# Spectra with real and imaginary parts on the rows, 16-bit phases, and the skip term by GpSimd and TensorE

## The chip, the core and the metric

One Trainium2 chip, of which the kernel uses one core. A core has five engines that run their own instruction queues in order: TensorE (PE, with its weight loads shown apart as PEld), VectorE (DVE), ScalarE (ACT), GpSimd (POOL) and SyncE (SP), which here only issues transfers. They meet through semaphores. The metric is the time of one execution on the device in microseconds.

## What is computed

The forward and the backward pass (the vector-Jacobian product for `grad_out`) of one block. `A_u` has 2048 rows of 512 in bf16; the state-space part has 128 states for each of the 512 channels; the dense part is 512 to 1792 to 512.

```python
def _A_ref(u, A_re, A_im, B_re, B_im, C_re, C_im, log_dt, Dskip):
    dt = jnp.exp(log_dt)[:, None]
    logdA = dt * (A_re + 1j * A_im)
    dB = dt * (B_re + 1j * B_im)
    P = jnp.exp(logdA[:, :, None] * l[None, None, :])
    K = jnp.einsum("dn,dnl,dn->dl", Cc, P, dB).real
    Kf, Uf = rfft2(pad(K)), rfft2(pad(u.transpose(0, 2, 1)))
    y = irfft2(Uf * Kf)[..., :L].transpose(0, 2, 1) + u * Dskip
    return y

xn = _layernorm(A_u)
s = _A_ref(xn, ...)
g = _silu(_silu(xn @ w1) @ w2)
out = A_u + s * g
```

The outputs are `out` and the gradients for `A_u`, the six state-space arrays, `log_dt`, `Dskip`, `w1` and `w2`.

## The kernel before

The convolution along the 2048 rows is done as a discrete Fourier transform by matmuls, in four blocks `b` of 128 channels. `dft_fwd` makes a spectrum in three steps: s1 (32 matmuls, line 298) over the first factor of the length, a turn by 32 PE transposes (line 304), and s2 (line 314) over the second. A spectrum is a tile of 128 rows x 4096: in the free direction `c` (real, imaginary), 16 groups `g` and 128 columns `k`. In s2 the real and the imaginary part come from two matrices of 64 columns, `F2[:, 0]` and `F2[:, 1]`; each matmul fills 64 rows of the PSUM tile, one group `h` on the upper and one on the lower half. `cplx_mul` (lines 340 to 354) multiplies two spectra on DVE, in two halves of five or six instructions with a help tile `cm2`. `dft_inv` goes back: i2 (line 327) with two accumulated matmuls for each group, 256 columns wide, and i1 (line 336) with two for each of the 16 steps `t`; a function `consume` takes each half of the result out of PSUM.

The stages stand in this order. The set-up loads x and the parameters, normalises, and builds constants (`make_consts`). Then `chain()` runs, block by block, the tables of the state-space kernel (`gen_tables`), the spectrum of x (`gen_conv_x`) and, one block behind, the forward convolution (`gen_conv_fwd`), while the dense forward pass (`gen_ffn_fwd`, ps_h and ps_o) is paced beside it. `gen_tables` makes its sines from integer phases `V`: a product (line 433), a shift by a quarter turn (435), a shift of bits (436) that throws away whole turns, and the sine on ACT (438). `gen_conv_fwd` reloads the spectrum of x (`spectrum_in`), stores its own (`KXd`), multiplies, and in `consume` adds the skip term xn * Dskip (lines 543, 544) on DVE. The last forward block runs beside the gates (`gen_gate_rows`). Then come the backward convolutions (`gen_conv_bwd`): `forward(b)` makes the spectrum `dA` of ds, and `rest(b)` loads both stored spectra and multiplies `dA` by each, with an inverse transform for each; the FFN's backward pass (`gen_ffn_da`, ps_da, dhT, ps_dx) and the output rows (`gen_out`) run beside it. The state-space gradients and the weight gradients follow.

The program is written as generators that are interleaved; a scheduler then orders each engine's queue by dependences and priority before the run, and at run time every queue is strict. Transfers are issued in order by SP (most), by GpSimd (stores of hT, ob and the outputs, `k.st`) and by ACT (a few). Spectra live in pool tiles with tag `w8` (4 buffers, and 2 more, `w8b`, in the backward stage); PSUM tiles for the convolutions (`pc`) have two buffers. `evc` casts on ACT (line 44), `evq` copies on DVE (line 45).

Of the kernel before, what the change touches and what calls it, by code (L numbers as in the profile page):

```python
# [14 lines left out]
I32 = mybir.dt.int32  # L15
DRAM = bass.MemoryType.DRAM
PSUM = bass.MemoryType.PSUM
P = 128
PI_LO = 3.1415925
PB = 18  # L20
# [113 lines left out]
def make_consts(k, wp):  # L134
# [11 lines left out]
    c8 = wp.tile([P, 16, 8], I32, name="c8")  # L146
    G.iota(c8[:], pattern=[[1, 16], [0, 8]], base=0, channel_multiplier=0)
    c4 = wp.tile([P, 16, 4], I32, name="c4")
    G.iota(c4[:], pattern=[[1, 16], [0, 4]], base=0, channel_multiplier=0)
    e8 = wp.tile([P, 16, 8], I32, name="e8")  # L150
    G.iota(e8[:], pattern=[[0, 16], [1, 8]], base=0, channel_multiplier=0)
# [21 lines left out]
    pt, ph, pe, pg = (wp.tile([P, 1], I32, name=nm) for nm in ("p_t", "p_h", "p_e", "p_g"))  # L173
# [4 lines left out]
    nc.vector.scalar_tensor_tensor(out=pg[:], in0=ph[:], scalar=4.0, in1=pe[:], op0=ALU.mult, op1=ALU.add)  # L178
# [4 lines left out]
    TT(out=kf[:, 0], in0=flat(c4), in1=pt[:].to_broadcast([P, 64]), op=ALU.mult)  # L183
    TT(out=kf[:, 1], in0=kf[:, 0], in1=sh[:, 1:2].to_broadcast([P, 64]), op=ALU.add)
    TT(out=kf[:, 0], in0=kf[:, 0], in1=sh[:, 0:1].to_broadcast([P, 64]), op=ALU.add)
    TS(out=kf[:], in_=kf[:], scalar=15, op=ALU.bitwise_and)
    kk = wp.tile([P, 128], I32, name="kk")
    TT(out=kk[:], in0=flat(c8), in1=pt[:].to_broadcast([P, 128]), op=ALU.mult)
    mask = wp.tile([P, 128], F32, name="mask")
    TT(out=mask[:], in0=flat(e8), in1=pg[:].to_broadcast([P, 128]), op=ALU.is_equal)  # L190
    maskf = wp.tile([P, 64], F32, name="maskf")
    TT(out=maskf[:], in0=flat(e4), in1=pe[:].to_broadcast([P, 64]), op=ALU.is_equal)
    kq = wp.tile([P, 3, 128], I32, name="kq")
    for i, shift in enumerate((12, 8, 0)):
        TS(out=kq[:, i], in_=kk[:], scalar=shift, op=ALU.add)
    TS(out=kq[:], in_=kq[:], scalar=15, op=ALU.bitwise_and)
    sf = wp.tile([P, 2, 64], F32, name="sf")
    nc.scalar.activation(out=sf[:], in_=kf[:], func=ACT.Sin, scale=2.0 * math.pi / 16.0, bias=k.mpi[:])
    sv = wp.tile([P, 3, 128], F32, name="sv")
    nc.scalar.activation(out=sv[:], in_=kq[:], func=ACT.Sin, scale=2.0 * math.pi / 16.0, bias=k.mpi[:])  # L200
# [6 lines left out]
    TT(out=sv[:], in0=sv[:], in1=mask[:].unsqueeze(1).to_broadcast([P, 3, 128]), op=ALU.mult)  # L207
    k.I2 = const.tile([P, 2, 2, 128], BF16, name="I2")
    TS(out=k.I2[:, 0], in_=sv[:, 0:2], scalar=2.0 / 4096, op=ALU.mult)
    TS(out=k.I2[:, 1, 0, :], in_=sv[:, 2], scalar=2.0 / 4096, op=ALU.mult)  # L210
    TS(out=k.I2[:, 1, 1, :], in_=sv[:, 0], scalar=2.0 / 4096, op=ALU.mult)
# [76 lines left out]
def dft_fwd(k, w8, U, ev):  # L288
# [19 lines left out]
    Bv = B[:].rearrange("p u (g h) k -> p u h g k", h=2)  # L308
    for u in range(2):
        for c in range(2):  # L310
            ps = pc.tile([P, 8, P], F32, name="ps_s2", tag="pc")
            for v in range(2):
                for h in range(2):
                    nc.tensor.matmul(out=ps[64 * h:64 * h + 64, 4 * v:4 * v + 4], lhsT=k.F2[:, c, :], rhs=Bv[:, u, h, 4 * v:4 * v + 4, :],  # L314
                                     start=True, stop=True)
            ev(A[:, c, 8 * u:8 * u + 8, :], ps[:])
# [3 lines left out]
def dft_inv(k, A2, Y, ev, consume):  # L320

    nc, pc = k.nc, k.pc
    for g0 in range(0, 16, 4):
        ps = pc.tile([P, 4, 32, 8], F32, name="ps_i2", tag="pc")
        for g in range(4):
            for c in range(2):
                nc.tensor.matmul(out=ps[:, g], lhsT=Y[:, c, g0 + g, :], rhs=k.I2[:, c].rearrange("p c m -> p (c m)"),  # L327
                                 start=(c == 0), stop=(c == 1))
        ev(A2[:].rearrange("p c t (g e) -> p g (c t) e", e=8)[:, g0:g0 + 4], ps[:])
    yield  # L330
    for h in range(2):
        ps = pc.tile([P, 8, P], F32, name="ps_i1", tag="pc")
        for j in range(8):
            t = 8 * h + j
            for c in range(2):
                nc.tensor.matmul(out=ps[:, j], lhsT=k.TI[:, 2 * t + c, :], rhs=A2[:, c, t, :], start=(c == 0), stop=(c == 1))
        consume(8 * h, 8, ps)


def cplx_mul(k, w8, a, b, conj=False):  # L340

    TT = k.nc.vector.tensor_tensor
    n = 8
    for g0 in range(0, 16, n):
        gs = slice(g0, g0 + n)
        t2 = w8.tile([P, 2, n, P], BF16, name="cm2", tag="cm2")
        TT(out=t2[:, 0], in0=b[:, 1, gs], in1=a[:, 1, gs], op=ALU.mult)
        TT(out=t2[:, 1], in0=b[:, 0, gs], in1=a[:, 1, gs], op=ALU.mult)
        TT(out=b[:, :, gs], in0=b[:, :, gs], in1=a[:, 0:1, gs].to_broadcast([P, 2, n, P]), op=ALU.mult)
        TT(out=b[:, 0, gs], in0=b[:, 0, gs], in1=t2[:, 0], op=ALU.add if conj else ALU.subtract)  # L350
        if conj:
            TT(out=b[:, 1, gs], in0=t2[:, 1], in1=b[:, 1, gs], op=ALU.subtract)
        else:
            TT(out=b[:, 1, gs], in0=b[:, 1, gs], in1=t2[:, 1], op=ALU.add)

# [155 lines left out]
def spectrum_in(k, w8, b, which):  # L511
    t = w8.tile([P, 2, 16, P], BF16, name="sp_in", tag="w8")
    k.nc.sync.dma_start(t[:].rearrange("p c g k -> p (c g k)"), {"U": k.Ud, "K": k.KXd}[which][b])
    return t
# [701 lines left out]
```

## Time and profile before

| | |
|---|---|
| median of 3 runs | 702.68 us (699.33 to 708.69) |
| span of the profiled execution | 703.6 us |
| PE busy | 597.5 us (85%) |
| DVE busy | 534.5 us (76%) |
| ACT busy | 465.3 us (66%) |
| GpSimd busy | 85.6 us (12%) |
| moved by DMA | 148.81 MB, 211 GB/s on average |
| mean granted TensorE clock | 0.958 |

Busy times are from the hardware profiler's record of one execution. The durations of single instructions are used from that execution, so sums are held against its span and not against the median. A matmul's mean duration includes the time through the array, in which the next is already running; the union of busy time divided by the count is nearer to what one costs. A busy share over the whole span mixes stages with different limits.

### The profile page before, as it was taken

To read this page: it belongs to the slowest core of one execution; us is meant where nothing else is said; L and a number is where in the kernel's file an instruction comes from. 1 tells how busy PE (TensorE), PEld (TensorE's weight loads), DVE (VectorE), ACT (ScalarE), POOL (GpSimd) and SP (SyncE) were. 2 spreads that over 40 slices of the span, in tenths; PEclk is the share of its full clock that TensorE was granted. 3 is DMA by queue.
4 is the path that set the end of the run, shared out by engine and by line. 5 is a ranking of instruction groups with operands and counts; after the bars stand their busy time and mean duration, and the time that the engine had idled before them with its cause. 6 is when DMAs were issued, how large, how long until landed. Compare 5 with 4: busy or idle time off the path is not lost.

```text
span 703.6 us, 14464 instructions
## 1 busy us (share of the span) xinstructions
PE 597.5 (85%) x5884; PEld 436.8 (62%) x5884; DVE 534.5 (76%) x952; ACT 465.3 (66%) x626; POOL 85.6 (12%) x165
## 2 busy tenths in 40 slices
PE   0675988779999997549988999988998989999988
PEld 0454656466667675337675666756777767755877
DVE  6988995979979958999685969626679774755950
ACT  6877666779878888877664765615728665645431
POOL 2355200000000000000000000000001020123220
PEclk9998998899999999779999999999999999999999
DMA  9955453825835779598857545479989999337993
GB/s 280 342 139 201 150 192 143 329 77 211 306 120 217 288 245 310 175 295 264 275 166 226 184 172 180 129 155 226 249 202 252 197 235 232 110 116 254 288 229 99
DMA packets 158771, 148.81 MB, mean 211 GB/s; under 512 B 79280, under 2 KB 136112, under 8 KB 155120
## 3 DMA queue, kind: packets, MB, share of 16 engines
q1 hardware_dynamic: 145664, 125.07, 62.3%
q0 software_dynamic: 6144, 17.83, 6.7%
q10 hardware_dynamic: 6896, 4.98, 2.2%
q8 instruction: 46, 0.75, 0.4%
q14 instruction: 21, 0.17, 0.1%
HBM read 65.14 MB, written 64.36 MB: 184 GB/s over the span
## 4 chain that ended last, share of the span: by engine, by line
issue 74%; POOL 8%; DVE 8%; PE 4%; DMA 4%; ACT 1%; SPq 0%; POOLq 0%; DVEq 0%
PE ps_w L986 2%; POOL Hd L575 1%; DMA dh_tok<-DHd 1%; DVE st L269 1%; POOL out_dram L842 1%; POOL rstd L273 1%; DVE jk L1019 1%; POOL SEL L220 1%; DVE o L1029 1%; DMA out_dram<-gout 1%; PE ps_o L583 1%; DMA out_dram<-o 1%; DVE xn L279 1%; POOL out_dram L971 1%; PE ps_h L566 1%
## 5 line engine op out<-in xcount | busy, mean ns | idle before, releaser
L44 ACT CAST dA<-ps_s 128x1024 bf16<-128x1024 f32 x96 | 93.6, 1027 | 16.2 <-PE ps_s L298 10.2
L925 PE MATMUL ps_da<-doT,W 128*128 128x256 bf16 x448 | 62.5, 280 | 5.7 <-DVE dhT L927 5.7
L44 ACT CAST dB<-ps_i 128x1024 bf16<-128x1024 f32 x48 | 47.3, 1027 | 29.2 <-PE ps_i L327 24.4
L772 DVE TENSOR_TENSOR Tp<-Vb,Eb 128x1344 bf16<-128x1344 bf16 x64 | 51.9, 853 | 18.5 <-ACT Vb L44 7.9
L927 DVE TENSOR_TENSOR dhT<-ps_da,dhT 128x512 bf16<-128x512 f32 x56 | 37.8, 686 | 34.2 <-PE ps_da L925 29.3
L566 PE MATMUL ps_h<-XT,W 128*128 128x256 bf16 x448 | 62.1, 284 | 0.6 <-DVE XT L45 0.4
L583 PE MATMUL ps_o<-W,aT 128*128 128x512 bf16 x224 | 56.9, 390 | 3.5 <-ACT aT L574 1.6
L327 PE MATMUL ps_i<-I,sp_in 128*128 128x256 bf16 x384 | 51.4, 279 | 8.0 <-DVE sp_in L350 4.9
L936 PE MATMUL ps_dx<-W,dhT 128*128 128x512 bf16 x224 | 54.1, 379 | 0.0
L925 PEld LDWEIGHTS <-W 128*128 128x128 bf16 x448 | 43.0, 100 | 16.7 <-issue 10.8
L986 PE MATMUL ps_w<-dh_tok,xn 128*128 128x256 bf16 x448 | 49.7, 272 | 3.6 <-DMA dh_tok<-DHd 3.5
L968 PE MATMUL ps_w<-YD,a_tok 128*128 128x512 bf16 x224 | 51.5, 379 | 0.0
L566 PEld LDWEIGHTS <-W 128*128 128x128 bf16 x448 | 43.2, 102 | 12.3 <-issue 5.5
L986 PEld LDWEIGHTS <-xn 128*128 128x128 bf16 x448 | 43.6, 98 | 9.8 <-issue 4.5
L327 PEld LDWEIGHTS <-sp_in 128*128 128x128 bf16 x384 | 36.7, 100 | 20.9 <-DVE sp_in L350 8.2
L44 ACT CAST Vb<-ps_v 128x672 bf16<-128x672 f32 x64 | 42.3, 725 | 10.7 <-PE ps_v L762 10.6
L44 ACT CAST o<-ps_w 128x256 bf16<-128x256 f32 (+1 forms) x42 | 17.7, 439 | 46.4 <-PE ps_w L986 16.9
L314 PE MATMUL ps_s<-dB,F 128*64 128x512 bf16 x192 | 33.6, 418 | 12.2 <-DVE dB L45 6.5
L298 PEld LDWEIGHTS <-TF 128*128 128x128 bf16 x384 | 26.7, 102 | 24.4 <-issue 18.6
L583 PEld LDWEIGHTS <-aT 128*128 128x128 bf16 x224 | 21.3, 100 | 29.4 <-issue 9.3
L45 DVE COPY dB<-pt_f 128x2048 bf16<-128x2048 bf16 x24 | 28.7, 1218 | 12.5 <-PE pt_f L304 12.4
L472 PE MATMUL ps_k<-W,YD 128*128 128x84 bf16 x512 | 29.4, 210 | 9.6 <-DVE W L467 7.7
(231 smaller groups left out, 1304.5 us busy)
## 6 DMA issues: line engine op xcount, KB each, us to landing
Yd<-YD SPq DMA_DIRECT2D x8, 1024.0 KB, 4.5
sp_in<-Ud SPq DMA_DIRECT2D x8, 1024.0 KB, 7.4
h_in<-Hd SPq DMA_DIRECT2D x14, 512.0 KB, 4.3
Ed<-E SPq DMA_DIRECT2D x8, 672.0 KB, 4.1
Eb<-Ed SPq DMA_DIRECT2D x8, 672.0 KB, 5.2
Hd<-hT POOLq DMA_DIRECT2D x8, 512.0 KB, 6.0
Ud<-dA SPq DMA_DIRECT2D x4, 1024.0 KB, 8.1
KXd<-dA SPq DMA_DIRECT2D x4, 1024.0 KB, 5.2
```

Source lines behind the costliest of these rows:

```text
L44: return self.nc.scalar.copy(out=out, in_=in_)
L314: nc.tensor.matmul(out=ps[64 * h:64 * h + 64, 4 * v:4 * v + 4], lhsT=k.F2[:, c, :], rhs=Bv[:, u, h, 4 * v:4 * v + 4, :], start=True, stop= ...
L327: nc.tensor.matmul(out=ps[:, g], lhsT=Y[:, c, g0 + g, :], rhs=k.I2[:, c].rearrange("p c m -> p (c m)"), start=(c == 0), stop=(c == 1))
L472: nc.tensor.matmul(out=ps[:, q], lhsT=Y[:, m % 2, q0 + 4 * u + q].rearrange("p j a -> p (j a)"), rhs=W[:, m, 4 * u + q].rearrange("p e a - ...
L566: nc.tensor.matmul(out=ps[:, j], lhsT=k.W1[:, dk, ft * P:ft * P + P], rhs=XTv[:, :, dk, :], start=(dk == 0), stop=(dk == DK - 1))
L583: nc.tensor.matmul(out=ps[:], lhsT=aT[:, ft, t * P:t * P + P], rhs=k.W2[:, ft, :], start=(ft == 0), stop=(ft == FT - 1))
L772: k.nc.vector.tensor_tensor(out=Tp[:, c, :, r ^ c].rearrange("p e (q w) a -> p q w e a", w=2), in0=Vb[:, :, c].rearrange("p q w (e a) -> p ...
L925: nc.tensor.matmul(out=ps[:, j], lhsT=k.W2[:, ft, dk * P:dk * P + P], rhs=dTv[:, :, dk, :], start=(dk == 0), stop=(dk == DK - 1))
L927: nc.vector.tensor_tensor(out=dh[:, i0:i0 + 2, :], in0=ps[:], in1=dh[:, i0:i0 + 2, :], op=ALU.mult)
L936: nc.tensor.matmul(out=ps[:], lhsT=dhs[ft // 8][:, ft % 8, t * P:t * P + P], rhs=k.W1[:, :, ft * P:ft * P + P], start=(ft == 0), stop=(ft ...
L968: nc.tensor.matmul(out=ps[:], lhsT=at[:, t, :], rhs=k.do[:, t, :], start=(t == 0), stop=(t == k.T - 1))
L986: nc.tensor.matmul(out=ps[:], lhsT=k.xn[:, t, dk * P:dk * P + P], rhs=dh[:, t].rearrange("p j n -> p (j n)"), start=(t == 0), stop=(t == k ...
```

## The change

Five things are done.

- The two matrices of s2 stand side by side as one of 128 columns, so that one matmul gives the real parts on rows 0 to 63 and the imaginary parts on rows 64 to 127. A spectrum is now 32 groups of 128 columns, each with both parts on the rows.
- A product of two spectra becomes two plain products on DVE: one with the spectrum as it is and one with a copy whose halves of rows are swapped. Sums and signs of the complex product are done by i2, whose matrix `I2` has two forms (`conj`) and which adds both products in PSUM: 64 matmuls of 128 columns for 32 of 256.
- The swapped copy is made by two transfers of 64 rows each: from the stored spectrum `Ud` in the forward blocks (`Us`), and from `dA` itself in the backward blocks (`As`).
- Phases have 16 bits (`PB` 16 for 18), and the sine reads the low half of each 32-bit word, so the shift of bits is gone; the two sines are separate instructions.
- The skip term is multiplied by GpSimd into `S`, brought into PSUM by a matmul with the identity (`plus`) ahead of i1, and the result is cast out by ACT.

With it, `cm2` goes, `w8` has 5 buffers and `w8b` 3, and the pool `p1` closes with the tables.

```diff
-PB = 18
+PB = 16
...
-    Bv = B[:].rearrange("p u (g h) k -> p u h g k", h=2)
-    for u in range(2):
-        for c in range(2):
-            ps = pc.tile([P, 8, P], F32, name="ps_s2", tag="pc")
-            for v in range(2):
-                for h in range(2):
-                    nc.tensor.matmul(out=ps[64 * h:64 * h + 64, 4 * v:4 * v + 4], lhsT=k.F2[:, c, :], rhs=Bv[:, u, h, 4 * v:4 * v + 4, :],
-                                     start=True, stop=True)
-            ev(A[:, c, 8 * u:8 * u + 8, :], ps[:])
+    for g0 in range(0, 32, 8):
+        ps = pc.tile([P, 8, P], F32, name="ps_s2", tag="pc")
+        for v in range(0, 8, 4):
+            nc.tensor.matmul(out=ps[:, v:v + 4], lhsT=k.F2[:].rearrange("p c n -> p (c n)"), rhs=Bf[:, g0 + v:g0 + v + 4], start=True, stop=True)
+        ev(Af[:, g0:g0 + 8], ps[:])
...
-def dft_inv(k, A2, Y, ev, consume):
+def dft_inv(k, A2, Y, conj, ev, consume, plus=None):
...
-    for g0 in range(0, 16, 4):
-        ps = pc.tile([P, 4, 32, 8], F32, name="ps_i2", tag="pc")
-        for g in range(4):
-            for c in range(2):
-                nc.tensor.matmul(out=ps[:, g], lhsT=Y[:, c, g0 + g, :], rhs=k.I2[:, c].rearrange("p c m -> p (c m)"),
-                                 start=(c == 0), stop=(c == 1))
+    for g0 in range(0, 32, 8):
+        ps = pc.tile([P, 8, 32, 4], F32, name="ps_i2", tag="pc")
+        for g in range(8):
+            for m in range(2):
+                nc.tensor.matmul(out=ps[:, g], lhsT=Y[m][:].rearrange("p c g k -> p (c g) k")[:, g0 + g],
+                                 rhs=k.I2[:, conj, m].rearrange("p c m -> p (c m)"), start=(m == 0), stop=(m == 1))
...
+            if plus is not None and j % 4 == 0:
+                nc.tensor.matmul(out=ps[:, j:j + 4], lhsT=k.ident[:], rhs=plus[:, t:t + 4], start=True, stop=False)
...
-def cplx_mul(k, w8, a, b, conj=False):
...
+def products(k, out, a, b):
+
+    for g0 in range(2):
+        k.nc.vector.tensor_tensor(out=out[:, g0], in0=a[:, g0], in1=b[:, g0], op=ALU.mult)
...
-            TS(out=V[:, 0, 0:n], in_=V[:, 1, 0:n], scalar=-float(1 << (PB - 2)), op=ALU.add)
-            TS(out=V[:, :, 0:n], in_=V[:, :, 0:n], scalar=32 - PB, op=ALU.logical_shift_left)
-            nc.scalar.activation(out=sn[:, :, 0:n], in_=V[:, :, 0:n], func=ACT.Sin, scale=-2 * PI_LO / 2.0 ** 32)
+            TS(out=V[1][:, 0:n], in_=V[0][:, 0:n], scalar=-float(1 << (PB - 2)), op=ALU.add)
+            for c in range(2):
+                low = V[1 - c][:].bitcast(I16).rearrange("p e (d w) -> p e d w", w=2)[:, 0:n, :, 0]
+                nc.scalar.activation(out=sn[:, c, 0:n], in_=low, func=ACT.Sin, scale=-2 * PI_LO / 2.0 ** PB)
...
+    if which[1:]:
+        k.nc.sync.dma_start(tf[0:64], src[64:P])
+        k.nc.sync.dma_start(tf[64:P], src[0:64])
...
-    cplx_mul(k, dft, KX, U)
+    products(k, U, KX, U)
+    products(k, Us, KX, Us)
     S = dft.tile([P, 16, P], BF16, name="S_b", tag="t4")
+    nc.gpsimd.tensor_tensor(out=S[:], in0=k.xn[:, :, bs], in1=k.Dbc[:, bs].unsqueeze(1).to_broadcast([P, 16, P]), op=ALU.mult)
     def consume(t0, n, ps):
-        xd = dft.tile([P, 8, P], BF16, name="xd", tag="cm2")
-        nc.vector.tensor_tensor(out=xd[:], in0=k.xn[:, t0:t0 + n, bs], in1=k.Dbc[:, bs].unsqueeze(1).to_broadcast([P, n, P]), op=ALU.mult)
-        nc.vector.tensor_tensor(out=S[:, t0:t0 + n], in0=ps[:], in1=xd[:], op=ALU.add)
-    yield from dft_inv(k, A2, U, k.evc, consume)
+        k.evc(S[:, t0:t0 + n], ps[:])
+    yield from dft_inv(k, A2, (U, Us), 0, k.evc, consume, S)
...
+        As = dft.tile([P, 2, 16, P], BF16, name="sp_s", tag="w8")
+        nc.sync.dma_start(flat(As)[0:64], flat(A)[64:P])
+        nc.sync.dma_start(flat(As)[64:P], flat(A)[0:64])
+        X = dft.tile([P, 2, 16, P], BF16, name="sp_x", tag="w8")
-        cplx_mul(k, dft, A, U, conj=True)
+        products(k, X, A, U)
+        products(k, U, As, U)
...
-        cplx_mul(k, dft, A, KX, conj=True)
+        products(k, As, As, KX)
+        products(k, KX, A, KX)
```

## The prediction

> **What bounds the kernel now.** I read the page first (PE busy 85%, DVE 76%, ACT 66%), then cut the span into the program's stages and asked for each engine's busy time in each, because an average over such different stages says nothing about one.
>
> ```profile
> 43.00:170.00 127.00, 102.57 (x1050) 73.92 (x1050) 107.89 (x149) 92.40 (x127) 26.63 (x30) 0.92 0.49 178
> 170.00:268.00 98.00, 94.87 (x1005) 66.08 (x1005) 83.76 (x115) 85.46 (x123) 7.70 (x10) 1.00 0.64 230
> 268.00:316.00 48.00, 27.18 (x278) 20.48 (x277) 45.84 (x82) 38.95 (x39) 1.12 (x2) 0.79 0.81 259
> 316.00:475.00 159.00, 145.57 (x1309) 104.02 (x1309) 114.97 (x160) 93.01 (x102) 5.94 (x11) 0.97 0.62 195
> ```
>
> The columns are the stretch, its length, then busy time of PE, PEld, DVE, ACT and POOL, the granted clock, the DMA share and GB/s. Before 43 us is the set-up, after 475 us the gradients of the state-space part and the weights; the change touches neither of them in weight. **B1** (43 to 170: tables and first convolutions) has no full engine: DVE is the busiest (107.9 of 127) and PE idles 24.4 us. **B2** (170 to 268, same work) is PE's: 94.9 of 98. **C** (268 to 316: last forward convolution and the gates) is DVE's: 45.8 of 48, while PE works 27 us. **D** (316 to 475: backward convolutions beside the FFN's backward pass) is again mostly PE's, 13.4 us idle.
>
> Next come the groups of instructions that the change touches:
>
> ```profile
> L349 DVE TENSOR_TENSOR sp_in<-sp_in,dA 128x2048 bf16<-128x2048 bf16 x24 | 29.3, 1221 | 0.3
> L347 DVE TENSOR_TENSOR cm<-sp_in,dA 128x1024 bf16<-128x1024 bf16 x24 | 16.4, 685 | 1.5 <-ACT dA L44 1.2
> ...
> L436 DVE TENSOR_SCALAR V<-V 128x2048 int32<-128x2048 int32 x8 | 9.9, 1231 | 0.0
> L544 DVE TENSOR_TENSOR S_b<-ps_i,xd 128x1024 bf16<-128x1024 f32 x8 | 9.8, 1220 | 8.5 <-PE ps_i L336 8.4
> ...
> L543 DVE TENSOR_TENSOR xd<-xn,Dbc 128x1024 bf16<-128x1024 bf16 x8 | 5.5, 687 | 0.1
> ...
> L314 PE MATMUL ps_s<-dB,F 128*64 128x512 bf16 x192 | 33.6, 418 | 12.2 <-DVE dB L45 6.5 <-ACT dB L44 2.9 <-ACT dA L44 2.6
> ...
> L336 PE MATMUL ps_i<-dB,TI 128*128 128x128 bf16 x384 | 23.9, 219 | 3.7 <-ACT dB L44 3.4 <-DVE dB L45 0.2
> ```
>
> The mean of a matmul includes its way through the array; busy time divided by count is the pace.
>
> **The products (DVE).** The complex product runs 12 times (4 forward, 8 backward). It goes: L349 29.3, L347, L348 and L350 16.4 each, L352 10.9, L354 5.5, together 94.9 us. In its place stand 12 x 4 plain products of 128x2048, the form of L349: 48 x 1.221 = 58.6. That is 36.3 less, 3.0 per call: 3.0 in B1, 6.1 in B2, 3.0 in C, 24.2 in D.
>
> **The phases (DVE, ACT).** The shift L436 goes: 8 x 1.231 + 8 x 1.165 = 19.2 us of DVE, some 11.5 in B1 and 7.7 in B2. The 16 sines become 32 of half the size; ACT takes 1.03 to 1.06 us for 1024 elements and 1.94 for 2048 (L438), so 16 x 0.15 = 2.4 us more. Reading 16-bit halves in steps of 4 bytes is in no row; the L169 sine reads int32 too and takes 2.0 us for 2048, so I bound it by 0 and +3 and take 0, since ACT's rows follow the count of elements. Halving the last bits of the phase changes no time.
>
> **The skip term.** L543 and L544 leave DVE: 15.3 us, 3.8 per block (B1 one, B2 two, C one). ACT gets 8 casts of 128x1024 at 1.027 (the row of dA<-ps_s): 8.2 us. PE gets 16 identity matmuls of 512 columns at the pace of ps_dx (54.1/224 = 0.24): 3.9. GpSimd gets 4 products of 2048 elements. Its product of 128 elements took 0.42 us, of which a fill of 64 (0.17) shows the fixed part: 0.17 + 16 x 0.25 = 4.2; sixteen whole ones are 6.7. I take 5. It does not come free for DVE:
>
> ```profile
> 52.98 1.58 POOL L220 TENSOR_SCALAR_AFFINE_SELECT SEL<-FO 128x512 bf16<-128x512 bf16 x1
> ...
> 53.38 1.57 DVE L446 TENSOR_TENSOR E<-sn,mag 128x1024 bf16<-128x1024 bf16 x1 [0.43 <-ACT sn L438]
> ```
>
> The same product of DVE has a median of 0.68 us; beside a GpSimd instruction that reads SBUF it lasted 1.57 and ended only after that one did. So each of the four can hold DVE between 0 and 5 us. About half of DVE's time goes to products with two SBUF inputs, so I take 2.5 each: 10 of the 15.3 come back. The Trainium skill's page "SBUF — State Buffer" (Who interferes with whom) says this outright: a VectorE instruction with two SBUF inputs and a GpSimd instruction that reads SBUF exclude each other for the whole instruction. By that rule all four would be paid in full, which is one of the rivals below; the trace's row agrees with it.
>
> On GpSimd the product stands between stores of hT and ob, each of which waits for ACT; the next block's stores wait behind it, 5 us, and GpSimd works only 34 us in all of B. On PE the first identity matmul waits for S_b, and everything on PE waits behind it; S_b needs only xn, so it is ready long before i1 unless a store ahead of it is late.
>
> **PE.** s2: four 64-column matmuls take 0.56 us from start to next start (344.86 to 345.42), two of 128 columns twice ps_dx's 0.22 there; 48 x 0.12 = 6 less. By busy time it is 33.6 - 96 x 0.24 = 10.4 less. Take 8. i2 has 768 matmuls of 128 columns for 384 of 256: at L336's pace 768 x 62 ns = 47.8 against 51.4; by undisturbed starts 2 x 1.79 us for 64 against 2 x 1.74 for 32, +1.2 over 12 calls. Take -1. With the identity matmuls PE loses 5 us (1 to 11).
>
> **The swapped copies.** New are 16 transfers of 64 partitions, 512 KB each: the U spectrum a second time (forward) and dA turned over (backward). Their 8 MB are 5% of 148.8 MB. SP issues each in 0.3 to 0.4 us, 16 x 0.4 = 6 us over 400 us, and the queue stands on waits, not on issues. The cost is the wait: the second product on DVE needs the copy, and behind it in DVE's queue stand dhT products that empty PE's ps_da. A 512 KB transfer lands in 3.9 us (Kb<-Kd), 1 MB of U in 7.4; so a pair takes 4 to 8 us, of which the first products cover 2.4. In forward blocks 0 to 2 it is covered: U was issued at 124.3 and used at 137.3. In C (issued 274.6, landed 8.6 later, used 284.2) and D, DVE has gates or dhT, and some 40 ps_da and ps_dx matmuls stand ahead of the first full group of i2. I take 0, with 0 to 8 for each of these five places.
>
> Set-up: two iotas of GpSimd (0.35 each) and a few DVE instructions of 64 to 128 elements leave, others come; all lie beside the loading of x. Nothing. Of the pools, one or two more spectrum buffers loosen waits for a slot; nothing counted.
>
> **The sum**, against the span of 703.6; the median of the three runs is 702.68, 0.9 below it. B1: DVE loses 11.5 + 3.0 + 3.8 - 2.5 = 15.8. It is the busiest engine there, but PE and ACT are close behind; two thirds show: -10.5 (-2 to -16). B2: PE is full, so only PE's own share (s2 -2.6, two blocks of identity +2, i2 -0.3) and a third of its 3.1 idle: -2 (0 to -6). C: DVE loses 3.0 + 3.8 - 2.5 = 4.3, and the stage is DVE's: -4 (-7 to +4). D: PE -3, and of 13.4 idle, of which PE waited 5.7 for dhT, 2: -5 (-12 to +32). Together -21.5: 703.6 - 21.5 - 0.9 = 681. Likeliest range 670 to 688.
>
> **The rivals.**
> - *Relief off the path.* ACT (177.9 us busy from 43 to 268, now 186) and PE set B1 as well; then DVE idles more: B1 -2, B2 -1, C -4, D -3, 693 us. For it: DVE stood 9.5 us waiting for pt_f around 115 us. Against: DVE is first in B1 by 5 us.
> - *GpSimd shuts DVE out.* Every skip product holds DVE for 5 or 6 us: +3 per block in B1 and C, and in B2 PE's identity matmul waits, +3: 681 + 9 = 690. The E row speaks for it; against it, DVE often reads PSUM or one operand. The Trainium skill's page "SBUF — State Buffer" (Who interferes with whom) gives this course.
> - *The copy takes the product's place: slower.* A backward block can't start its copy before dA's slot is free, its second half stands behind dUd in SP's queue, and i2 now needs both sets of products for its first group. If each of the five uncovered places pays 8 us (a pair that lands one after the other, as 1 MB of U took up to 9.8), 681 + 40 = 721. It decides from 7.1 us a place, where 681 + 5 x 7.1 reaches 716.7. Against: B of the next block runs beside it. The Trainium skill's page "SBUF — State Buffer" ("Can I just issue two DMAs to hit both halves?") says that two transfers on the two halves of the partitions serialize; no row here shows one of 64 partitions.
> - *All of it shows.* B1 -16, B2 -6, C -7, D -12: 662 us. PE's clock, 0.79 in C, would rise with fewer pauses.
>
> **How the numbers follow.** Chances: the forecast 0.48, all of it 0.12, relief off the path 0.13, GpSimd 0.12, the copies 0.15. A difference of 2% (14 us: below 688.6 or above 716.7) is about what a measurement can tell here, with runs from 699.3 to 708.7. Faster: 0.48 + 0.12 = 0.60; within: 0.25; slower: 0.15. The range 660 to 710 takes in all but the copies.
>
> **What would show it.** DVE's total near 535 - 71 + 10 = 474 us and ACT's near 476; s2 x96 with some 23 us; i2 x768 near 50. In C less than 45 us with DVE not full; PE idle in B1 under 15 us. Wrong would be: DVE products beside GpSimd's of 3 us and more; DVE or PE idle with the swapped copy as releaser, over 3 us a place; PE idle in B1 still 24.

## The result and the profile after

The kernel after takes 726.86 us (median of 4, 722.98 to 729.9) against 705.2 us for the kernel before in the same runs (699.33 to 708.69): ratio 1.030, 95% interval 1.024 to 1.035. It is slower; 681 was forecast. Its profiled execution has a span of 726.3 us. Ratios, here and below, compare only the fast executions of two kernels; beside e13 to e16 nine of before's 17 executions counted as slow, and beside e5 to e8 three of ten, so that there the ratios lie 0.3 to 1.1 per cent above the quotients of the medians.

To set the two side by side I cut both at four events that each kernel has: the last kernel-table group (ps_e), the first and the last transform of ds, the last ps_da. The busy table of after in these stretches (stretch, length, then busy time of PE, PEld, DVE, ACT, POOL, granted clock, DMA share, GB/s):

```profile
43.00:255.80 212.80, 187.59 (x1981) 138.08 (x2001) 157.79 (x212) 172.91 (x254) 42.38 (x43) 0.94 0.62 217
255.80:305.00 49.20, 33.74 (x340) 26.60 (x341) 36.05 (x58) 37.74 (x49) 4.74 (x2) 0.79 0.68 222
305.00:408.60 103.60, 82.11 (x882) 64.15 (x885) 61.88 (x80) 67.20 (x70) 4.91 (x9) 0.92 0.83 253
408.60:535.60 127.00, 113.21 (x1150) 86.58 (x1149) 72.71 (x87) 66.35 (x82) 1.57 (x3) 0.97 0.78 193
535.60:726.30 190.70, 171.96 (x1711) 131.01 (x1721) 117.82 (x308) 95.80 (x151) 31.30 (x56) 0.97 0.85 194
```

The same table of before:

```profile
43.00:256.40 213.40, 186.13 (x1947) 132.29 (x1947) 186.51 (x256) 168.16 (x232) 34.33 (x40) 0.95 0.56 202
256.40:299.60 43.20, 30.44 (x309) 21.71 (x306) 35.13 (x61) 35.95 (x46) 0.57 (x1) 0.88 0.70 226
299.60:396.90 97.30, 81.01 (x764) 58.90 (x764) 78.33 (x115) 66.63 (x69) 4.92 (x9) 0.91 0.75 239
396.90:518.80 121.90, 112.54 (x1048) 83.27 (x1046) 82.10 (x110) 66.14 (x82) 1.57 (x3) 0.99 0.73 188
518.80:703.60 184.80, 170.37 (x1724) 129.47 (x1721) 117.51 (x308) 95.55 (x151) 31.29 (x56) 0.99 0.82 200
```

So B (tables, first convolutions) changed by -0.6 us, C (last forward block, gates) by +6.0, D (both middle rows, backward convolutions) by 230.6 - 219.2 = +11.4, the rest by +5.9. In B and D DVE lost 28.7 and 25.8 us of work (186.5 to 157.8, 160.4 to 134.6), and neither became shorter. The groups of after that answer to those shown of before (sp_in is a loaded spectrum or its swapped copy, sp_s the swapped copy of dA, and sp_x takes the first product of a backward block):

```profile
L323 PE MATMUL ps_i<-I,sp_in 128*128 128x128 bf16 x512 | 51.7, 231 | 11.9 <-DVE sp_in L342 10.3 <-ACT dK L45 0.9 <-ACT dB L45 0.3
...
L342 DVE TENSOR_TENSOR sp_in<-dA,sp_in 128x2048 bf16<-128x2048 bf16 x24 | 28.3, 1218 | 4.6 <-DMA sp_in<-Ud 4.6
...
L311 PE MATMUL ps_s<-dB,F 128*128 128x512 bf16 x85 | 25.6, 378 | 3.4 <-ACT dA L45 2.2 <-DVE dB L46 0.7
...
L536 POOL TENSOR_TENSOR S_b<-xn,Dbc 128x2048 bf16<-128x2048 bf16 x4 | 16.5, 4130 | 25.2 <-DMA Sd<-S_b 25.2
...
L342 DVE TENSOR_TENSOR sp_in<-sp_s,sp_in 128x2048 bf16<-128x2048 bf16 x8 | 9.4, 1219 | 8.9 <-DMA sp_s<-dA 8.9
...
L423 DVE TENSOR_SCALAR V<-V 128x960 int32<-128x960 int32 x8 | 8.5, 1059 | 0.1
...
L434 DVE TENSOR_TENSOR E<-sn,mag 128x320 bf16<-128x320 bf16 x16 | 7.9, 491 | 14.2 <-ACT sn L426 14.2
```

The products cost what was forecast (1.218 us each), and the shift is gone. New are waits for transfers before products (4.6 and 8.9 us), and V<-V of 960 elements takes 1059 ns on average where in before (line 435) it took 663. DVE also stands longer for the sines within B; here is before, then after (waited for: us in total, times, longest):

```profile
DVE E L446 <- ACT sn L438: 7.3, 8, 2.8
...
DVE E L434 <- ACT sn L426: 20.4, 8, 6.6
```

### The profile page after: what moved, and what is told of

The parts are those of the page before. It is cut to its first block, busy times and chain, and to the rows that moved or that the text cites. A ratio compares the mean times of both kernels' runs of the same rounds, so it can differ in the third digit from the quotient of the medians.

```text
span 726.3 us, 14989 instructions
## 1 busy us (share of the span) xinstructions
PE 606.6 (84%) x6145; PEld 458.0 (63%) x6188; DVE 481.3 (66%) x849; ACT 472.1 (65%) x650; POOL 94.2 (13%) x167
## 5 line engine op out<-in xcount | busy, mean ns | idle before, releaser
L929 DVE TENSOR_TENSOR dhT<-ps_da,dhT 128x512 bf16<-128x512 f32 x56 | 37.4, 685 | 47.7 <-PE ps_da L927 30.7
L927 PE MATMUL ps_da<-doT,W 128*128 128x256 bf16 x448 | 62.3, 281 | 7.2 <-DVE dhT L929 4.7
L561 PE MATMUL ps_h<-XT,W 128*128 128x256 bf16 x448 | 63.9, 290 | 1.3 <-DVE XT L46 0.8
L45 ACT CAST dB<-ps_i 128x1024 bf16<-128x1024 f32 x48 | 47.9, 1037 | 21.5 <-PE ps_i L323 21.5
L323 PE MATMUL ps_i<-I,sp_in 128*128 128x128 bf16 x512 | 51.7, 231 | 11.9 <-DVE sp_in L342 10.3
L988 PE MATMUL ps_w<-dh_tok,xn 128*128 128x256 bf16 x448 | 52.3, 282 | 6.9 <-DMA dh_tok<-DHd 6.9
L988 PEld LDWEIGHTS <-xn 128*128 128x128 bf16 x448 | 45.2, 101 | 14.1 <-issue 7.4
L927 PEld LDWEIGHTS <-W 128*128 128x128 bf16 x448 | 43.8, 101 | 15.9 <-issue 8.1
L323 PEld LDWEIGHTS <-sp_in 128*128 128x128 bf16 x512 | 42.6, 104 | 17.7 <-DVE sp_in L342 13.8
L561 PEld LDWEIGHTS <-W 128*128 128x128 bf16 x448 | 45.2, 104 | 13.3 <-issue 1.8
L970 PE MATMUL ps_w<-YD,a_tok 128*128 128x512 bf16 x211 | 49.2, 379 | 0.8 <-issue 0.2
L578 PEld LDWEIGHTS <-aT 128*128 128x128 bf16 x224 | 22.2, 104 | 33.7 <-issue 12.8
L46 DVE COPY dB<-pt_f 128x2048 bf16<-128x2048 bf16 x24 | 28.9, 1217 | 15.1 <-PE pt_f L303 15.1
L45 ACT CAST hT<-ps_h 128x512 bf16<-128x512 f32 x56 | 32.8, 610 | 7.8 <-PE ps_h L561 7.8
L426 ACT ACTIVATE sn<-V 128x1024 bf16<-128x1024 int16 (+1 forms) x32 | 33.6, 1067 | 3.2 <-DVE V L423 3.2
```

What stands on the lines that cost most here:

```text
L45: return self.nc.scalar.copy(out=out, in_=in_)
L46: return self.nc.vector.tensor_copy(out=out, in_=in_)
L323: nc.tensor.matmul(out=ps[:, g], lhsT=Y[m][:].rearrange("p c g k -> p (c g) k")[:, g0 + g], rhs=k.I2[:, conj, m].rearrange("p c m -> p (c ...
L426: nc.scalar.activation(out=sn[:, c, 0:n], in_=low, func=ACT.Sin, scale=-2 * PI_LO / 2.0 ** PB)
L561: nc.tensor.matmul(out=ps[:, j], lhsT=k.W1[:, dk, ft * P:ft * P + P], rhs=XTv[:, :, dk, :], start=(dk == 0), stop=(dk == DK - 1))
L578: nc.tensor.matmul(out=ps[:], lhsT=aT[:, ft, t * P:t * P + P], rhs=k.W2[:, ft, :], start=(ft == 0), stop=(ft == FT - 1))
```

## The experiments

The times below are medians of 6 to 12 executions (after: 4); "before" ran beside them at 702 to 705. The table has each kernel's ratio to before and the lengths of its stages in its one profiled execution (B counted from the start; the times of one kernel spread over some 1 per cent, so a few us in one stage are no finding by themselves).

| run | ratio (95%) | median us | B | C | D | rest |
|---|---|---|---|---|---|---|
| before | 1 | 702 to 705 | 256.4 | 43.2 | 219.2 | 184.8 |
| after | 1.030 (1.024-1.035) | 726.9 | 255.8 | 49.2 | 230.6 | 190.7 |
| e1 phases | 0.994 (0.990-0.997) | 698.0 | 247.4 | 42.8 | 220.2 | 181.9 |
| e2 skip term | 1.013 (1.009-1.018) | 711.4 | 257.2 | 48.3 | 223.0 | 185.1 |
| e3 spectra | 1.034 (1.030-1.039) | 727.4 | 256.7 | 46.3 | 240.4 | 184.5 |
| e4 after, no copies | 1.023 (1.018-1.027) | 718.9 | 255.0 | 48.3 | 227.0 | 187.5 |
| e5 after, casts on DVE | 1.027 (1.021-1.033) | 717.7 | 251.3 | 46.1 | 233.0 | 180.4 |
| e6 skip, GpSimd half | 1.018 (1.012-1.024) | 712.9 | 261.8 | 44.4 | 222.7 | 185.6 |
| e7 skip, PE and ACT half | 1.013 (1.008-1.018) | 709.7 | 255.9 | 45.6 | 220.6 | 185.3 |
| e8 spectra, no copies | 1.024 (1.019-1.030) | 716.8 | 257.7 | 43.1 | 229.1 | 182.7 |
| e9 after, rows later | 1.021 (1.015-1.027) | 717.1 | 254.8 | 47.7 | 227.6 | 179.9 |
| e10 before, rows later | 1.000 (0.997-1.003) | 703.4 | 255.1 | 42.6 | 219.6 | 186.7 |
| e11 skip, order only | 1.009 (1.006-1.012) | 707.7 | 256.9 | 42.8 | 224.4 | 187.6 |
| e12 spectra and phases | 1.016 (1.012-1.020) | 712.9 | 246.2 | 48.7 | 230.3 | 183.2 |
| e13 phases and skip | 1.022 (1.015-1.029) | 711.3 | 257.3 | 47.2 | 221.7 | 185.0 |
| e14 e12, rows later | 1.014 (1.006-1.022) | 706.6 | 248.2 | 48.2 | 229.5 | 180.8 |
| e15 e14, copies by ACT | 1.038 (1.031-1.045) | 723.6 | 246.2 | 47.4 | 246.1 | 185.6 |
| e16 e14, no copies | 0.997 (0.993-1.001) | 696.8 | 246.6 | 43.1 | 226.0 | 178.8 |
| e17 after, product on DVE | 1.002 (0.998-1.005) | 704.5 | 245.8 | 49.6 | 221.3 | 187.4 |
| e18 after, sum on DVE | 1.027 (1.022-1.033) | 722.6 | 253.5 | 48.3 | 234.0 | 183.8 |

### The three parts alone

e1 is before with the 16-bit phases:

```diff
-            TS(out=V[:, :, 0:n], in_=V[:, :, 0:n], scalar=32 - PB, op=ALU.logical_shift_left)
+                low = V[1 - c][:].bitcast(I16).rearrange("p e (d w) -> p e d w", w=2)[:, 0:n, :, 0]
```

> The kernel before with the 16-bit phases alone: DVE loses its 16 shifts (19.2 us), ACT takes 32 half-size sines. The forecast's own step put two thirds of DVE's relief in the first tables stage: some 8 us off, ratio near 0.988. My theory now, from the trace of after, where DVE lost 29 us between 43 and 256 us and the last kernel-table product came 1.5 us sooner, is that DVE sets no end there: 0 to 3 us off, ratio 0.996 to 1.0. Rival: the strided 16-bit reads cost ACT more than the rows showed and it gets slower by 3 us or more.

e2 is before with the skip term in its new form:

```diff
+    nc.gpsimd.tensor_tensor(out=S[:], in0=k.xn[:, :, bs], in1=k.Dbc[:, bs]..., op=ALU.mult)
-        nc.vector.tensor_tensor(out=S[:, t0:t0 + n], in0=ps[:], in1=xd[:], op=ALU.add)
+        k.evc(S[:, t0:t0 + n], ps[:])
```

> The kernel before with the skip term alone by GpSimd, identity matmuls and ACT casts. DVE loses 15.3 us. Theory: nothing is gained, since identity matmuls (5 us) and casts (8 us) go to the engines that are full: 0 to +4 us, ratio 1.0 to 1.006. Rival: this part is where the 22 us went, through DVE shut out beside GpSimd and PE standing behind the identity matmul: +10 us or more, ratio over 1.014. The forecast had about -4 us for it.

e3 is after with shift and skip term back on DVE (the product written into S, then S = ps + S):

> The change's spectra alone (both parts on the rows, swapped copies, products summed in the inverse transform), with the shift back on DVE and the skip term back on DVE. Theory: the loss sits here, +15 to +24 us, ratio 1.02 to 1.034, with the backward stage 8 to 12 us longer. The forecast had DVE -36 and PE -9 here, some -9 us in time. Rival (loss in the skip term): +2 to +8 us.

The phases gain 0.65 per cent, by a B that is 9.0 us shorter:

```profile
43.00:247.40 204.40, 185.62 (x1926) 132.38 (x1940) 168.43 (x239) 168.79 (x249) 30.07 (x40) 0.96 0.58 210
```

DVE works 18.1 us less there than in before and half of it shows in that stage, so my theory behind the result (DVE sets no end there) fell, and the forecast's step fits the stage. The median is only 4.0 us lower, half of the 8 that the step would give; the profiled execution was e1's fastest (694.0). The skip term costs 9 us (between the two expectations) and the spectra 25. The three don't add: 9 + 25 - 4 = 30, and after is 22 above before. This version, e1, is the one that beats both kernels.

### The copies

e4 is after without the 16 swapped transfers, e8 is e3 without them; the second products take unswapped spectra, so the convolutions' outputs are other numbers:

```diff
-    U, Us = (spectrum_in(k, dft, b, w) for w in ("U", "Us"))
+    U = spectrum_in(k, dft, b, "U")
...
-        nc.sync.dma_start(flat(As)[0:64], flat(A)[64:P])
-        nc.sync.dma_start(flat(As)[64:P], flat(A)[0:64])
-        products(k, U, As, U)
+        products(k, U, A, U)
```

> The kernel after without the 16 swapped transfers: the second products take the unswapped spectra, so the convolutions' outputs are other numbers; tiles, products and matmuls are as many as in after. If the copies (their waits and what they hold up on the SP queue) are the loss: back to 700 to 707 us, ratio 0.995 to 1.005. If the order of work or PE's share is the loss, and the copies are hidden: 718 to 727, ratio over 1.02. By the forecast's sum without its errors it would stand at 681.

> The spectra alone (shift and skip term on DVE) without the 16 swapped transfers; the second products take unswapped spectra, so the convolutions' outputs are other numbers. Between after and the same without copies 5 to 8 us lay. If the copies cost about that here too: ratio 1.02 to 1.027, and most of the spectra's 24 us is not the copies. If they are the whole: 0.99 to 1.005.

By the medians the copies cost 8.0 us in after and 10.6 in the spectra alone (0.7 and 1.0 per cent by the ratios): more than the 0 forecast, and not the whole loss.

### The skip term's halves, and the order of work

e6 keeps GpSimd's product in e2 and sums on DVE; e7 keeps identity matmuls and casts and multiplies on DVE; e11 multiplies and sums on DVE, but the product stands ahead of the inverse transform:

```diff
 # e6
-        k.evc(S[:, t0:t0 + n], ps[:])
+        nc.vector.tensor_tensor(out=S[:, t0:t0 + n], in0=ps[:], in1=S[:, t0:t0 + n], op=ALU.add)
 # e7
-    nc.gpsimd.tensor_tensor(out=S[:], ...)
+    for t0 in (0, 8):
+        nc.vector.tensor_tensor(out=S[:, t0:t0 + 8], ...)
```

> The kernel before with the skip term's product on GpSimd, the sum still on DVE (S = ps + S): no identity matmuls, no casts on ACT. If GpSimd's product (DVE shut out, stores behind it) is the 9 us that the skip term cost: ratio 1.010 or more. If the identity matmuls and casts are it: 0.995 to 1.004.

> The kernel before with the skip term's product on DVE, summed by identity matmuls and cast by ACT; nothing new on GpSimd. If identity matmuls and casts are the 9 us: ratio 1.010 or more. If GpSimd is: 0.997 to 1.004. If both halves come out near 1.0, the loss is in how the order of work falls when the two are together.

> The kernel before with the skip term's product written straight into S_b ahead of the inverse transform, on DVE, and the sum on DVE as before: the same instructions, one tile (xd) less, another order. If any new order of work costs this kernel about 1 per cent, the two halves of the skip term were slower for the order alone: ratio 1.007 or more. If the halves cost by their own instructions: 0.996 to 1.004.

Each half costs as much as the whole, and e11, with not one instruction more, costs 0.9 per cent. So in before, without the phases, these runs can't tell a half's price from that of a new order: the scheduler had laid out the queues anew in each. e5 moves the 48 casts of dB (the inverse transform's first stage) from ACT to DVE in after; the same is done at the two calls of the backward convolution:

```diff
-    yield from dft_inv(k, A2, (U, Us), 0, k.evc, consume, S)
+    yield from dft_inv(k, A2, (U, Us), 0, k.evq, consume, S)
```

> The kernel after with the 48 casts of the inverse transform's first stage (dB from ps_i, 1.03 us each on ACT) moved to DVE (1.2 us each), which the change left idle a third of the time. If after's first stage is held by ACT's queue (DVE's waits for the sines grew from 7 to 20 us there), 43 to 256 us shrinks by 5 us or more and the whole by 8 or more: ratio below 1.02. If DVE's late products and loads hold it, DVE gets later still: ratio 1.03 or more.

B is 4.5 us shorter in the profile and the median 9 us lower, but the ratio, 1.027 after 1.030, hardly moved and fell between the two expectations. How much of this is a gain is open.

### The backward stage

After's waits in the first part of D (305 to 409 us; engine, line, waited for, us in total, times, longest):

```profile
DVE go_g L650 <- DMA go_g<-Gd: 20.3, 4, 9.5
...
DVE sp_in L342 <- DMA sp_s<-dA: 5.5, 1, 5.5
```

DVE stands with a side task, the output rows (go_g, go_x), at the head of its queue. What stands behind it is seen in its timeline (start, duration, instruction, and idle time before it with what ended it):

```profile
344.21 0.69 DVE L650 TENSOR_TENSOR go_g<-go_g,go_s 128x1024 bf16<-128x1024 bf16 x1
354.35 0.69 DVE L650 TENSOR_TENSOR go_g<-go_g,go_s 128x1024 bf16<-128x1024 bf16 x1 [9.46 <-DMA go_g<-Gd]
355.78 0.69 DVE L651 TENSOR_TENSOR go_x<-go_x,go_g 128x1024 bf16<-128x1024 bf16 x1 [0.74 <-DMA go_x<-in_A_u_dram]
...
360.74 0.69 DVE L650 TENSOR_TENSOR go_g<-go_g,go_s 128x1024 bf16<-128x1024 bf16 x1 [3.14 <-DMA go_g<-Gd]
...
362.49 1.22 DVE L700 TENSOR_TENSOR du_b<-ps_i,dsd 128x1024 bf16<-128x1024 f32 x1
```

du_b empties a PSUM tile, and PE waits for it:

```profile
363.76 1.01 PE L297 MATMUL ps_s<-ds,TF 128*128 128x128 bf16 x8 [5.01 <-DVE du_b L700]
```

The load that landed before 354.35 had been issued at 346.00, behind a store on SP's queue (Pd) that had waited 2.7 us for ACT. e9 takes the output rows out of the backward stage's pacing in the program, e10 does so in before:

```diff
-    paced(bwd, woven([ffb, out], [2, 1]), BR)
+    paced(bwd, ffb, BR * 2 / 3)
```

> The kernel after with the output rows (go_g, go_x: 16 DVE products and 24 loads on the SP queue) taken out of the backward stage and run behind it. In after DVE stands 28 us in that stage at the head of its queue for these loads, and PE then waits 8 us for du_b. If that standing is what lengthened the stage: ratio 1.01 to 1.02, the stage (first product of ds to last ps_da, 230.6 us) 10 us or more shorter, and more than the kernel before gains by the same move. If the stage is long for its own products and PE's waits: ratio 1.027 or more.

> The kernel before with the same move of the output rows. DVE stood 10.5 us for those loads there. If the move is worth the same to both kernels, it is no cause of the difference: before would then gain as much as after does. By my theory: within 3 us of before, ratio 0.995 to 1.005.

The medians fell by 9.8 us in after (0.9 per cent by the ratios) and by nothing in before. But the traces show that the edit does not take the rows out of D: the scheduler laid them back into it. In e10 they run from 312.7 to 397.2 us, in before from 312.3 to 403.4. In e9 they run from 343.6 to 435.2, in after from 315.4 to 409.1, and DVE stands even longer before them, 33.7 us against 28.3. So e9 is another order of the same work, what made it faster is not shown, and e10 does not test the rows. e12 is after with the skip term back on DVE; e14 adds e9's edit to it. e15 is e14 with the eight backward copies issued from ACT's queue, and e16 is e14 without all 16 copies, as in e4:

```diff
 # e15
-        nc.sync.dma_start(flat(As)[0:64], flat(A)[64:P])
+        nc.scalar.dma_start(flat(As)[0:64], flat(A)[64:P])
```

> The kernel after with the skip term back on DVE (product into S_b, then the sum). If the parts add: spectra +25, phases -4, so +21 and ratio 1.03; the skip term then added nothing to after. If the skip term costs here what it costs alone (9 us): +15, ratio 1.021.

> Spectra and phases, skip term on DVE, and the output rows taken behind the backward stage. Spectra and phases alone took 712.9; the move gave the kernel after 9.8 us and the kernel before nothing. If the loads of the output rows at the head of DVE's queue are what the spectra cost in the backward stage: 701 to 706, ratio 1.0 to 1.006, the backward stage near 222 us. If not: 710 to 713.

> As the run before it, with the eight swapped copies of the backward stage issued from ACT's queue, where dA is written, instead of SP's, behind whose waits and loads they stood. If waiting in SP's queue is their price: 2 to 6 us less than the run before it. If their price is the bytes (the DMA engines were 98 per cent busy around the waits of after): within 2 us of it, or worse.

> As two runs before, without the 16 swapped copies (the second products take unswapped spectra, so the convolutions' outputs are other numbers). What is left against phases alone (698) is the new form itself: products, i2 and s2. If the form costs nothing, or saves: 690 to 699. If it costs 8 us or more in the backward stage without copies and without the rows: 704 or more, and the backward stage stays over 226 us.

By e12 the skip term costs after 14 us (1.4 per cent by the ratios). In e14 the rows run from 339.4 to 432.3 us, still in D, and D is 229.5 us where 222 was expected had the rows' loads been its price; the time, 706.6, fell between the two expectations. So neither e9 nor e14 shows that these loads make D long. e15 was a miss: 17 us worse. ACT's queue issued the second pair of copies no sooner (359.4 and 366.5 us against 349.9 and 352.6 in e14), so it is no clean test of SP's queue either. e16 against e14 prices the copies at 9.8 us, 5.1 of them in C. There the four products follow each other in e16,

```profile
275.18 4.86 DVE L342 TENSOR_TENSOR sp_in<-dA,sp_in 128x2048 bf16<-128x2048 bf16 x4
```

and in after those on the copy come 4.8 us behind those on the spectrum, with gates in between:

```profile
287.19 1.22 DVE L342 TENSOR_TENSOR sp_in<-dA,sp_in 128x2048 bf16<-128x2048 bf16 x1 [0.49 <-DMA sp_in<-Ud]
...
288.93 1.22 DVE L342 TENSOR_TENSOR sp_in<-dA,sp_in 128x2048 bf16<-128x2048 bf16 x1
...
293.69 2.35 DVE L342 TENSOR_TENSOR sp_in<-dA,sp_in 128x2048 bf16<-128x2048 bf16 x2
```

In this order and without copies, spectra and phases stand where the phases alone stand (696.8 and 698.0): the new form need not cost anything. That it costs nothing is not shown, since e8, the form without copies and phases in another order, is 14 us above before. None of these runs shows a gain from it.

### Which half of the skip term

e13 is before with phases and the whole new skip term (e1 and e2 together). e17 is after with the product on DVE, e18 after with the sum on DVE (the edits of e7 and e6).

> The kernel before with the 16-bit phases and the skip term by GpSimd, identity matmuls and ACT casts; the spectra as before. Phases alone gave -4 us and 9 us in the stage up to 256 us. If the skip term takes just what the phases free there (its matmuls and casts go to PE and ACT, which set that stage once DVE is relieved): the stage is back at 253 to 257 us, time 709 to 714, ratio 1.01 to 1.017. If the skip term's loss needs the new spectra too: 700 to 706.

> The kernel after with the skip term's product on DVE instead of GpSimd; identity matmuls and ACT casts stay. Without the skip's new form the first stage ended at 246 us, with it at 256. If the matmuls and casts (PE 4 us, ACT 6 us in that stage) make the 9 us: the stage ends at 253 to 257 and the time is 722 to 728. If GpSimd's product does (DVE held beside it, 9.7 us in four places): it ends at 246 to 250, time 712 to 718.

> The kernel after with GpSimd's product kept and the sum on DVE (S = ps + S): no identity matmuls, no casts of S_b on ACT. The other half: if the matmuls and casts make the 9 us, the first stage ends at 246 to 250, time 712 to 718; if GpSimd's product does, at 253 to 257, time 722 to 728. If both halves end near 255, either suffices to eat the relief; if both near 248, it takes the two together.

e13 loses the relief of B again (257.3 after e1's 247.4), without any spectra. e17, one product for each block moved from GpSimd to DVE, takes 22 us off and is level with before (B came as expected for that cause, the time below the 712 to 718 expected with it); e18 keeps the loss. The stage B separates cleanly: with phases and GpSimd's product it ends at 251.3 to 257.3 (after, e4, e5, e9, e13, e18), with phases and without that product at 245.8 to 248.2 (e1, e12, e14 to e17). e17's table:

```profile
43.00:245.80 202.80, 182.54 (x1982) 134.84 (x2001) 155.08 (x217) 171.35 (x253) 30.01 (x40) 0.97 0.64 224
245.80:295.40 49.60, 31.40 (x337) 23.17 (x339) 36.16 (x66) 38.37 (x48) 0.75 (x1) 0.83 0.80 260
295.40:396.20 100.80, 82.88 (x899) 64.44 (x900) 61.33 (x77) 67.43 (x70) 4.91 (x9) 0.95 0.84 261
396.20:516.70 120.50, 109.11 (x1138) 83.89 (x1137) 70.80 (x86) 66.45 (x82) 1.57 (x3) 0.99 0.74 190
```

ACT's work in B is nearly after's (171.4 against 172.9), and DVE, which now multiplies too, is busy for 2.7 us less.

The edit moved the order of B as well: of some 319 instructions on DVE up to its end, 55 stand elsewhere in e17 than in after. A closer pair is e18 and e12, which differ only in who makes the product and when. Their DVE queues in B agree in all but 9 of some 212 other instructions, and in D in all of them. With the product on GpSimd B ends at 253.5, with it on DVE at 246.2, and the medians are 722.6 and 712.9: at nearly the same order, the four products cost 9.7 us (1.2 per cent by the ratios), 7.3 of them in B.

What GpSimd does to DVE is in after's timelines. First GpSimd:

```profile
89.61 4.21 POOL L536 TENSOR_TENSOR S_b<-xn,Dbc 128x2048 bf16<-128x2048 bf16 x1
...
150.31 4.05 POOL L536 TENSOR_TENSOR S_b<-xn,Dbc 128x2048 bf16<-128x2048 bf16 x1 [5.90 <-DMA Sd<-S_b]
...
268.86 4.19 POOL L536 TENSOR_TENSOR S_b<-xn,Dbc 128x2048 bf16<-128x2048 bf16 x1 [19.32 <-DMA Sd<-S_b]
```

then DVE in the same moments:

```profile
90.42 3.91 DVE L423 TENSOR_SCALAR V<-V 128x960 int32<-128x960 int32 x1
95.41 0.33 DVE L434 TENSOR_TENSOR E<-sn,mag 128x320 bf16<-128x320 bf16 x1 [1.07 <-ACT sn L426]
...
152.46 2.10 DVE L434 TENSOR_TENSOR E<-sn,mag 128x320 bf16<-128x320 bf16 x1 [5.03 <-ACT sn L426]
...
213.48 1.23 DVE L46 COPY dB<-pt_f 128x2048 bf16<-128x2048 bf16 x1 [7.85 <-PE pt_f L303]
...
269.18 4.42 DVE L621 TENSOR_TENSOR YD<-YD,u 128x1024 bf16<-128x1024 bf16 x1
```

V<-V took 3.91 us for 0.66, E 2.10 for 0.33, the gate 4.42 for 0.68, and each ended within 0.6 us of GpSimd's end; the copy out of PSUM beside the third product (213.36 to 217.43) took its usual 1.23. The held V is the input of a sine, and ACT stood for it:

```profile
ACT sn L426 <- DVE V L423: 3.2, 2, 2.9
```

ACT stands 6.2 us for V in B of e18 and not once in e17. That DVE's own standing for the sines follows from it is not shown: it is 20.4 us in after and 11.1 in e17, but 4.4 in e18. The Trainium skill's page "SBUF — State Buffer" (Who interferes with whom) has the rule that a VectorE instruction with two SBUF inputs and a GpSimd instruction that reads SBUF, and likewise a VectorE instruction in a two-port mode (which `tensor_scalar` can enter) and GpSimd, shut each other out: whoever issues first holds the shared ports for its whole instruction. These rows agree with it.

In D GpSimd does the same little work in after and e17 (6.5 us in both), so what is left there is the order. DVE's queue from the first dhT on has the same instructions in the same order in after, e3, e12 and e18; their D takes 230.6, 240.4, 230.3 and 234.0. In e17 the scheduler ordered the same work otherwise (some 45 of 147 instructions stand elsewhere), and D takes 221.3. That is one profile, 9.0 us under the lowest of four that differ by 10.1 among themselves, and which part of the order does it is open: e9 and e14, whose order in D is nearer to e17's (128 of 149 instructions agree), take 227.6 and 229.5. In e17 du_b stands ahead of the second sp_x, and no go_g waits long before it:

```profile
346.88 0.69 DVE L651 TENSOR_TENSOR go_g<-go_g,go_s 128x1024 bf16<-128x1024 bf16 x1 [1.46 <-issue]
347.49 1.22 DVE L701 TENSOR_TENSOR du_b<-ps_i,dsd 128x1024 bf16<-128x1024 f32 x1
348.63 1.22 DVE L342 TENSOR_TENSOR sp_x<-dA,sp_in 128x2048 bf16<-128x2048 bf16 x1
```

## Why the prediction was wrong, point by point

In these cuts the forecast was -12.5 us in B, -4 in C, -5 in D and nothing behind; the profiles have -0.6, +6.0, +11.4 and +5.9. (The forecast's own C and D were cut elsewhere, at 268, 316 and 475 us, so the split is rough.)

- **Products, phases, totals: right.** DVE's total was to be 474 us and is 481, ACT's 476 and is 472; the products cost 1.218 us, GpSimd's 4.13 (4.2 to 6.7 forecast, 5 taken).
- **Relief in B: right, and then lost.** Forecast -10.5 and -2; e1 gives -9.0 and e17 -10.6.
- **GpSimd's product: the step that failed first.** The forecast had DVE held 2.5 us each time. It was 3.2, 1.8, 1.0 and 3.7, in all 9.7 for 10 forecast, so the size was right. What failed is what the forecast did with it: it set the hold off against DVE's saved work and let two thirds of the rest show. With the product on GpSimd all of B's relief went, 7.3 us for three products at nearly the same order (e18 against e12) and some 10 against e17 and e1; DVE was held for 6.0 us in B of after. In the whole, the product costs 9.7 us at that order and 22 with the order that came with it. That a held instruction delays what waits for it is seen in ACT's 2.9 us before a sine; the rest of that chain is argued. The rival "GpSimd shuts DVE out" had this price (3 us a block) and gave it to the wrong total, since it left the rest of the gain in place.
- **Order of the later stage: not in the forecast.** The other half of e17's 22 us lies behind B: D is 9.3 us shorter in another order of the same work. The forecast took D's order as given. The two orders differ in one pair of kernels that differ in the product alone (after and e17), but e12, without GpSimd's product, has the longer one too, so the product is not what it hangs on. What in the order costs the time stays open.
- **Copies: 0 taken, 8 to 11 us measured** by the medians (5 to 12 by the ratios), in the profiles 0.9 to 5.1 in C and 3.5 to 11.3 in D: about 2 us for each of the five places. In B, where the forecast held the copies covered, DVE stood 4.1 us for U's loads and their copies. The mechanism was the one bounded (0 to 8 each). A 64-row transfer of 512 KB landed in 9.8 us (median) in after, while 1 MB over 128 rows took 8.1; the forecast had 4 to 8 for a pair. The rival's rule in the Trainium skill's "SBUF — State Buffer" ("Can I just issue two DMAs to hit both halves?"), that transfers on the two halves serialize, fits these landings: in all eight pairs the second half landed 1.3 to 3.4 us behind the first. But the halves were issued 0.5 to 3.0 us apart, and the four pairs that stand right behind another load of 1 MB in the queue took 9.9 to 12.4 us to land, the four others 4.4 to 9.8, so that part of it is the queue. At 2 us a place the copies do not reach the 7.1 from which the rival decided; its 8 us were taken from a landing of 9.8, which in before is a load of KXd (U's took up to 8.6).
- **C: forecast -4, came +6.0.** The forecast called C DVE's and had DVE lose 4.3 us there. In these cuts DVE was busy for 35.1 of 43.2 us before and for 36.1 after, so no relief came. e16 without copies and GpSimd's product has 43.1, just as before; with the copies C is 3.1 to 5.5 longer than before (e3, e12), with the new skip term 4.0 to 5.1 (e2, e13), with both 6.0 (after).
- **D: forecast -5, came +11.4.** DVE's 25.8 us less bought nothing that shows: PE is busy there for 193.6 us before and 195.3 after, and even without copies and GpSimd's product D takes 226.0 (e16) against 219.2. This is the largest miss, and beyond copies and order its cause stays open.
- **PE: forecast -5, came about +3.** i2's union of busy time went from 51.4 to 54.1 us (forecast -1); s2's 85 recorded of 96 matmuls take 25.6, so by an estimate 28.9 for all, -4.7 (forecast -8); the identity matmuls take 5.3 (forecast 3.9).
- **The rest: forecast nothing, +5.9.** In the other kernels it lies between 178.8 and 187.6. In after all of it lies behind 664 us (62.3 us for 56.4 in before), where PE waits 6.9 us for loads of dh_tok, 3.5 in before; the remainder was not followed up.

So three terms of the forecast failed. DVE's relief was to show as -21.5 us net of every cost; without GpSimd's product the change is worth nothing (e17, 1.002), as B's 10.6 us are given back in C, D and behind. The GpSimd product was taken as 2.5 us of DVE's time each, two thirds of which would show in B1; it took away all that B had gained. The copies were taken as 0 and cost 8 to 11 us. What brought D its other price is known only as far as the order of e17 shows it.

## What to carry to other kernels

Before handing work to GpSimd, look at which DVE instructions will run beside it, and do not price a held one by DVE's busy time alone; in this kernel four products of 4 us cost 9.7 us at nearly the same order of work, and 22 with the order that came with them. Where a scheduler lays out strict queues, an edit changes the order of stages that it does not touch: 0.9 per cent came and went here with no change in work (e11), so an edit worth less than that is judged with neutral variants beside it. Before the time of an edit that is meant to move work is read, the trace must show that the work moved (in e9 and e10 it did not leave its stage). A load for a side task at the head of the queue that empties PSUM made PE wait 5.0 us in one place here; what taking it away is worth no run shows.

## What the hardware showed that was not expected

The exclusion goes the other way too, and further. In e2 GpSimd's first product lasted 13.2 us in place of 4.05:

```profile
104.33 13.20 POOL L544 TENSOR_TENSOR S_b<-xn,Dbc 128x2048 bf16<-128x2048 bf16 x1
```

DVE ran its products one after the other through most of that time at their usual lengths (W 0.85, YD 0.95 us). In e18 one lasted 10.7 us beside such a stream. So here a stream of DVE work without a gap kept GpSimd waiting through many instructions, not one.

Groups of interleaved instructions can't be added up. After's i2 stands in three groups of 51.7, 17.4 and 15.5 us, together 84.6; in the timeline each matmul of sp_in starts while its neighbour of sp_x or sp_s still runs, and the union is 54.1.
